# One of five convolution taps of fourteen gates made on ScalarE and added by an accumulating transfer

## The chip, the cores and the metric

The kernel runs on one core of one Trainium2 chip, with TensorE (PE), VectorE (DVE), ScalarE (ACT), GpSimd (POOL) and SyncE (SP) working from queues of their own. The metric is the device time of one launch in microseconds (us). Everything is float32.

## The reference

The first half is linear attention for 8 batches and 8 heads: kv = k^T v for each head, out = q kv, and each row of out is divided by its root mean square and scaled by g_norm. The heads side by side make x with 576 tokens and 512 channels a batch. The second half is a gated linear unit whose gate is a causal convolution over five tokens:

```
xp = np.concatenate([np.zeros((B, K - 1, D)), x], axis=1)      # K = 5
for k in range(K):
    gate_pre += conv_w[k][None, None, :] * xp[:, k:k + S, :]
gate = 1.0 / (1.0 + np.exp(-gate_pre))
val = x @ w_val
return gate * val @ w_out
```

## The kernel before, in words

The whole order of the work is written out by hand in a string, PLAN: 1151 steps such as `gate_tap 2 0 3`, each a small function, called one after the other. Every engine works its own instructions in that order, and waits by semaphores for what the others make. So a step that waits holds all that stands behind it on its engine.

For a batch b, k and v come by two half loads (SP's queue), and kv_product makes kv on TensorE. raw_pair (L500) and raw_product multiply q with it into PSUM, two chunks of 128 tokens at a time in one PSUM tile, `raws`, which the next pair writes again. square (L524, ScalarE) and sums (L533, VectorE) make the sums of squares, powers (L543, GpSimd) the inverse roots, and normalise (L564, ScalarE, eight instructions a chunk, L572) writes x, emptying the PSUM tile. turn_blocks (L600, VectorE) transposes x in 32x32 blocks, and move_blocks (L603) moves them by four transfers of 64 KB, issued by GpSimd at L608, into xT, where channels lie on partitions. There are two xT tiles, for even and odd batches. halo (L612, GpSimd) copies the four border columns that the convolution needs.

For each block jt of 128 channels there is then one gate, 128 partitions by 576 tokens, 288 KB, in one of three buffers:

- gate_start (L617, ScalarE): the tap of the current token, x times a weight a partition;
- gate_tap for taps 3, 2, 1 and 0 (L623, VectorE, one instruction at L625): gate = x shifted * weight + gate;
- gate_end (L630, ScalarE, L632): the sigmoid, in place;
- gated (L648, VectorE, L650): gv = gv * gate, which also sets the gate's buffer free.

Meanwhile TensorE makes x @ w_val. For batches 2 to 7 that is val_fast (L673), seven groups of products in three PSUM banks, with sums of x made by x_sums (L662, VectorE); val_keep (L691) copies or adds the banks into gv, by ScalarE (L696 to L708) or VectorE (L694). Some of the groups add to a bank that val_keep has just copied. The output products (out_product, L718 and L725; fast_product, L784) read gv, keep_out and fast_keep empty their banks, and store writes the result from SP's queue.

Transfers issued by GpSimd use eight semaphores in turn; one that takes a semaphore waits until the transfer eight before it has landed. The steps that the change touches stand in the plan like this, gate 2 of batch 2 as the example (dots for steps between):

```
x_sums 2 1; gate_start 2 2; normalise 3 4; gate_tap 2 2 3; ... gate_tap 2 2 2; ... gate_tap 2 2 1; ...
powers 4 3; ... load_half v 5 1; gate_tap 2 2 0; ... powers 4 2; ... gate_end 2 2; ... normalise 4 2; ... gated 2 2
```

Of the kernel before, what the change touches and what calls it, by code (L numbers as in the profile page):

```python
# [15 lines left out]
P = 128  # L16
# [3 lines left out]
load_q_rows 0 1; stage_weight cw 0; load_q_rows 0 0; load_half v 0 0; load_half k 0 0; load_half v 0 1;  # L20
load_half k 0 1; warm_up; stage_weight wval 1; stage_weight wval 0; start_warm 36; turn_q_rows 0 0;
turn_q_rows 0 1; narrow_weight cw 0 0; turn_q_rows 0 2; narrow_weight cw 0 1; narrow_weight cw 0 2; sort_q 0 0;
turn_q_rows 0 3; sort_q 0 1; turn_q_rows 0 4; narrow_weight cw 0 3; kv_product 0 0; sort_q 0 2;
load_q_rows 1 0; narrow_weight cw 0 4; narrow_weight cw 0 5; load_half k 1 0; sort_q 0 3; narrow_weight cw 0 6;
load_half v 1 0; narrow_weight cw 0 7; sort_q 0 4; load_q_rows 1 1; load_half k 1 1; stage_weight wval 2;
keep_warm 2; kv_product 0 1; stage_weight wval 3; turn_cw; load_half v 1 1; kv_copy 0; keep_cw;
narrow_weight wval 1 0; raw_product 0 3; load_half v 2 0; raw_product 0 2; square 0 3; raw_product 0 4;
sums 0 3; stage_weight wout 0; square 0 2; raw_product 0 1; square 0 4; powers 0 3; sums 0 2;
narrow_weight wval 1 1; sums 0 4; raw_product 0 0; load_half v 2 1; square 0 1; narrow_weight wval 0 0;
narrow_weight wval 0 1; powers 0 2; square 0 0; normalise 0 3; sums 0 1; turn_x 0 3; sums 0 0; keep_x 0 3;  # L30
powers 0 4; normalise 0 2; narrow_weight wval 1 2; narrow_weight wval 1 3; turn_x 0 2; normalise 0 4;
turn_q_rows 1 0; roots 0; keep_x 0 2; narrow_weight wval 0 2; turn_x 0 4; sort_q 1 0; turn_q_rows 1 1;
keep_x 0 4; narrow_weight wval 0 3; normalise 0 1; turn_q_rows 1 2; halo 0; sort_q 1 1; normalise 0 0;
turn_x 0 1; narrow_weight wval 1 4; kv_product 1 0; narrow_weight wval 0 4; keep_x 0 1; sort_q 1 2;
narrow_weight wval 0 5; turn_x 0 0; narrow_weight wval 1 5; narrow_weight wval 0 6; turn_q_rows 1 3;
keep_x 0 0; narrow_weight wval 0 7; gate_start 0 0; turn_q_rows 1 4; narrow_weight wval 1 6; kv_product 1 1;
sort_q 1 3; load_q 2 0; narrow_weight wval 1 7; gate_start 0 1; narrow_weight wval 2 0; val_product 0 0 1;
gate_start 0 2; narrow_weight wval 3 0; sort_q 1 4; load_q 2 1; gate_tap 0 2 3; kv_copy 1; gate_tap 0 0 3;
narrow_weight wval 3 1; raw_product 1 3; narrow_weight wval 2 1; gate_tap 0 1 3; load_half k 2 0;
raw_product 1 2; keep_val 0 0 1; gate_tap 0 0 2; square 1 3; narrow_weight wval 3 2; val_product 0 1 1;  # L40
sums 1 3; square 1 2; gate_tap 0 1 2; powers 1 3; narrow_weight wval 2 2; load_half k 2 1; gate_tap 0 2 2;
narrow_weight wval 2 3; stage_weight wout 2; raw_product 1 1; sums 1 2; narrow_weight wval 3 3;
narrow_weight wval 2 4; raw_product 1 0; keep_val 0 1 1; powers 1 2; square 1 1; narrow_weight wval 2 5;
normalise 1 3; val_product 0 0 0; load_q 2 2; gate_tap 0 0 1; sums 1 1; turn_q 2 0; normalise 1 2; powers 1 1;
turn_x 1 3; narrow_weight wval 3 4; val_product 0 1 0; narrow_weight wval 2 6; keep_x 1 3; load_q 2 3;
narrow_weight wval 3 5; square 1 0; narrow_weight wval 2 7; normalise 1 1; turn_x 1 2; sums 1 0;
raw_product 1 4; gate_tap 0 2 1; stage_weight wout 1; powers 1 0; kv_product 2 0; narrow_weight wout 0 0;
square 1 4; sums 1 4; narrow_weight wout 0 1; narrow_weight wval 3 6; kv_product 2 1; keep_x 1 2; turn_q 2 1;
powers 1 4; normalise 1 0; gate_tap 0 2 0; turn_x 1 1; load_q 3 0; val_product 0 2 1; narrow_weight wval 3 7;
keep_x 1 1; gate_tap 0 1 1; keep_val 0 1 0; narrow_weight wout 0 2; gate_tap 0 1 0; keep_val 0 0 0; turn_x 1 0;  # L50
normalise 1 4; gate_tap 0 0 0; val_product 0 2 0; narrow_weight wout 2 0; narrow_weight wout 0 3; keep_x 1 0;
narrow_weight wout 0 4; kv_copy 2; val_product 0 3 1; turn_q 2 2; keep_val 0 2 1; keep_val 0 2 0; turn_q 2 3;
narrow_weight wout 2 1; load_q 3 1; gate_end 0 0; narrow_weight wout 0 5; turn_x 1 4; narrow_weight wout 0 6;
raw_pair 2 3; keep_val 0 3 1; keep_x 1 4; gated 0 0; narrow_weight wout 2 2; stage_weight wout 3; halo 1;
val_product 1 0 1; narrow_weight wout 0 7; load_q 3 2; square 2 3; square 2 2; sums 2 3;
narrow_weight wout 2 3; sums 2 2; powers 2 3; gate_end 0 1; val_product 1 0 0; narrow_weight wout 1 0;
gate_end 0 2; narrow_weight wout 2 4; gate_start 0 3; gated 0 1; keep_val 1 0 1; narrow_weight wout 2 5;
powers 2 2; load_half v 3 1; val_product 1 1 1; normalise 2 3; gate_tap 0 3 3; load_half k 3 0;
load_half v 3 0; turn_q 3 0; narrow_weight wout 2 6; val_product 0 3 0; normalise 2 2; gated 0 2;
narrow_weight wout 2 7; turn_blocks 2 3; narrow_weight wout 1 1; load_q 3 3; raw_pair 2 1; gate_tap 0 3 2;  # L60
narrow_weight wout 1 2; narrow_weight wout 3 0; raw_product 2 4; keep_val 1 0 0; turn_q 3 1; square 2 1;
val_product 1 1 0; load_half k 3 1; keep_val 0 3 0; sums 2 1; narrow_weight wout 3 1; gate_tap 0 3 1;
square 2 0; powers 2 1; square 2 4; sums 2 0; narrow_weight wout 3 2; val_product 1 2 1; gate_tap 0 3 0;
keep_val 1 1 1; narrow_weight wout 1 3; turn_blocks 2 2; powers 2 0; narrow_weight wout 3 3;
narrow_weight wout 1 4; val_product 1 2 0; normalise 2 1; turn_q 3 2; narrow_weight wout 3 4; load_q 4 1;
normalise 2 0; narrow_weight wout 3 5; val_product 1 3 1; narrow_weight wout 3 6; sums 2 4; load_q 4 0;
keep_val 1 1 0; narrow_weight wout 3 7; powers 2 4; gate_end 0 3; turn_blocks 2 1; kv_product 3 0;
gate_start 1 0; narrow_weight wout 1 5; keep_val 1 2 1; gated 0 3; normalise 2 4; val_product 1 3 0;
narrow_weight wout 1 6; gate_start 1 1; gate_tap 1 0 3; narrow_weight wout 1 7; turn_x 2 4; kv_product 3 1;
turn_blocks 2 0; keep_x 2 4; gate_start 1 2; gate_tap 1 0 2; move_blocks 2 3; keep_val 1 3 0; out_product 0 1;  # L70
turn_q 3 3; load_half k 4 1; kv_copy 3; load_half k 4 0; gate_tap 1 2 3; keep_val 1 3 1; keep_val 1 2 0;
gate_tap 1 1 3; gate_tap 1 0 1; gate_tap 1 1 2; raw_pair 3 3; gate_tap 1 0 0; gate_tap 1 1 1; out_product 0 0;
square 3 3; move_blocks 2 2; gate_tap 1 2 2; keep_out 0 1; gate_end 1 0; store 0 1; sums 3 3; square 3 2;
gate_tap 1 2 1; gated 1 0; powers 3 3; load_q 4 2; sums 3 2; out_product 0 3; keep_out 0 0; gate_tap 1 1 0;
gate_start 1 3; gate_tap 1 2 0; powers 3 2; gate_end 1 1; gate_tap 1 3 3; normalise 3 3; gate_tap 1 3 2;
move_blocks 2 1; store 0 0; out_product 0 2; gate_tap 1 3 1; gate_end 1 2; normalise 3 2; gated 1 1;
gate_tap 1 3 0; load_half v 4 0; halo 2; gated 1 2; gate_end 1 3; val_sums 0; raw_pair 3 1; keep_out 0 2;
gated 1 3; keep_out 0 3; turn_blocks 3 3; store 0 2; raw_product 3 4; square 3 1; val_sums 1; out_product 0 5;
square 3 0; move_blocks 2 0; turn_q 4 0; load_half v 4 1; sums 3 1; turn_blocks 3 2; val_sums 2; powers 3 1;
load_q 4 3; sums 3 0; out_product 0 7; turn_q 4 1; keep_out 0 5; square 3 4; powers 3 0; turn_q 4 2;  # L80
load_q 5 0; normalise 3 1; weight_sums 0; sums 3 4; val_sums 3; powers 3 4; normalise 3 0; out_product 0 4;
turn_blocks 3 1; x_sums 2 0; x_sums 2 1; gate_start 2 2; normalise 3 4; gate_tap 2 2 3; gate_start 2 0;
turn_blocks 3 0; kv_product 4 0; turn_q 4 3; gate_tap 2 2 2; kv_product 4 1; x_sums 2 3; turn_x 3 4;
x_sums 2 2; kv_copy 4; load_half k 5 1; val_fast 2 0 0; store 0 5; gate_tap 2 2 1; keep_x 3 4; raw_pair 4 3;
move_blocks 3 3; val_keep 2 0 0; val_fast 2 0 1; store 0 3; square 4 3; square 4 2; sums 4 3; val_fast 2 0 2;
gate_start 2 1; sums 4 2; powers 4 3; val_fast 2 0 3; load_half k 5 0; gate_tap 2 1 3; val_keep 2 0 2;
# [773 lines left out]
```

## Time and profile before

| what | us |
|---|---|
| median of 2 runs | 314.65 (313.96 and 315.34) |
| span of the profiled execution, first to last instruction | 313.7 (the page gives no other time of it) |
| granted TensorE clock in it | 1.000 |
| one tap on VectorE (L625), mean of 128 | 0.810 |
| one gate_start on ScalarE (L619), mean of 32 | 0.796 |
| issue of one 64 KB move on GpSimd (L608), mean of 96 | 0.556 |
| landing of such a move after its issue, least / median / most | 1.9 / 3.4 / 7.7 |

The profile shows one execution. Times of instructions count from the start of the span. For each group of instructions it gives the busy time, the mean of one and the idle time of the engine before them. The chain is followed back from the last instruction, at each step to what released it. A timeline lists instructions in order of time, runs of alike ones merged.

### The profile page before, as it was taken

What the parts mean: (1) busy time and instruction counts of PE and PEld (TensorE: products, weight loads), DVE (VectorE), ACT (ScalarE), POOL (GpSimd) and SP (SyncE); (2) the same over time, 40 slices, a digit from 0 to 9 for tenths busy, and PEclk for the clock granted to TensorE, in tenths of its full rate; (3) what the DMA queues carried; (4) which work ended last, traced back from release to release, by engine and by line L of the source; (5) the groups of instructions that cost most, each with busy time, mean ns of one, the idle gap of its engine ahead of it and who ended that gap; (6) DMA issues with size and microseconds to landing.
All of it is one profiled execution on the core that took longest, in us unless ns stands there. A gap on an engine that the chain in (4) does not pass through costs nothing.

```text
span 313.7 us, 8362 instructions
## 1 busy us (share of the span) xinstructions
PE 302.8 (97%) x3197; PEld 217.6 (69%) x3197; DVE 255.7 (82%) x462; ACT 191.1 (61%) x542; POOL 133.4 (43%) x175
## 2 busy tenths in 40 slices
PE   7978999999999999999999999999999999999993
PEld 7866878777645485757666776587668868888582
DVE  1149899999999969899999899899998999764412
ACT  1457899999485867747685858485773343352120
POOL 3033073435588456666684659265749000000000
PEclk9999999999999999999999999999999999999999
DMA  7999597599677769668966986422335213022322
GB/s 276 377 386 352 149 294 219 173 298 239 186 189 210 210 188 342 196 168 276 270 155 194 251 251 160 118 50 54 100 78 127 58 25 88 0 67 57 89 73 85
DMA packets 26696, 55.50 MB, mean 177 GB/s; under 512 B 6166, under 2 KB 8214, under 8 KB 26656
## 3 DMA queue, kind: packets, MB, share of 16 engines
q1 hardware_dynamic: 22608, 46.61, 49.8%
q0 software_dynamic: 3168, 6.32, 7.9%
q10 hardware_dynamic: 880, 2.03, 1.9%
q8 instruction: 25, 0.41, 0.5%
q14 instruction: 15, 0.12, 0.1%
HBM read 39.21 MB, written 9.44 MB: 155 GB/s over the span
## 4 chain that ended last, share of the span: by engine, by line
PE 85%; ACT 5%; DMA 4%; DVE 2%; SPq 1%; issue 1%; POOL 1%; ACTq 0%; DVEq 0%
PE out L718 18%; PE va L687 15%; PE a L784 8%; PE vc L687 8%; PE cb L784 6%; PE val L637 6%; PE raw L438 5%; PE out L725 5%; PE raw L510 4%; PE vb L687 4%; PE qTps L472 3%; PE raw L493 2%; DMA k<-in_k_dram 2%; DMA qs<-in_q_dram 2%; PE xTps L587 1%; ACT x L572 1%
## 5 line engine op out<-in xcount | busy, mean ns | idle before, releaser
L625 DVE SCALAR_TENSOR_TENSOR gate<-xT,cwT,gate 128x576 f32<-128x576 f32 x128 | 101.0, 810 | 2.1 <-ACT gate L619 1.6
L546 POOL TENSOR_TENSOR rt<-ss,mhalf 128x8 f32<-128x8 f32 (+1 forms) x38 | 65.4, 1728 | 80.7 <-DVE ss L540 77.1
L608 POOL DMA_DIRECT2D xT<-y x96 | 52.8, 556 | 17.4 <-DVE xs L671 6.0
L718 PE MATMUL out<-wout,gv 128*128 128x512 f32 x128 | 57.3, 595 | 0.0
L572 ACT ACTIVATE x<-raw,rt 128x64 f32<-128x64 f32 x252 | 55.3, 369 | 2.2 <-POOL rt L546 1.6
L718 PEld LDWEIGHTS out<-wout,gv 128*128 128x128 f32 x128 | 23.9, 190 | 26.0 <-issue 24.1
L637 PE MATMUL val<-xT,wval 128*128 128x288 f32 x128 | 32.9, 409 | 0.1
L540 DVE TENSOR_REDUCE ss<-sq 128x8 f32<-128x520 f32 (+1 forms) x38 | 23.3, 626 | 8.3 <-ACT sq L528 8.1
L528 ACT ACTIVATE sq<-raw 128x512 f32<-128x512 f32 (+1 forms) x40 | 21.6, 564 | 12.4 <-PE raw L510 8.8
L637 PEld LDWEIGHTS val<-xT,wval 128*128 128x128 f32 x128 | 23.6, 190 | 6.3 <-ACT xT L594 0.3
L619 ACT ACTIVATE gate<-xT,cwT 128x576 f32<-128x576 f32 x32 | 25.2, 796 | 4.0 <-DVE gv L650 3.9
L687 PE MATMUL va<-xs,vsum 128*128 128x288 f32 x96 | 27.2, 406 | 0.0
L650 DVE TENSOR_TENSOR gv<-gv,gate 128x576 f32<-128x576 f32 x32 | 24.2, 762 | 3.0 <-ACT gate L632 2.8
L632 ACT ACTIVATE gate<-gate 128x576 f32<-128x576 f32 x32 | 22.1, 702 | 5.5 <-DVE gate L625 5.4
L687 PEld LDWEIGHTS va<-xs,vsum 128*128 128x128 f32 x96 | 18.2, 190 | 4.7
L733 ACT COPY ot<-out 128x512 f32<-128x512 f32 x20 | 12.0, 603 | 14.0 <-PE out L725 6.0
L438 PEld LDWEIGHTS raw<-v,k 64*64 64x64 f32 x1008 | 15.5, 135 | 4.7 <-issue 3.8
L793 DVE TENSOR_TENSOR ot<-cb,ot 128x256 f32<-128x256 f32 x16 | 6.7, 420 | 14.7 <-ACT ot L797 7.0
L615 POOL COPY xT<-xT 128x124 f32<-128x124 f32 x32 | 13.4, 456 | 10.3 <-ACT xT L594 10.3
L708 ACT COPY gv<-va 128x288 f32<-128x288 f32 x12 | 4.8, 400 | 19.8 <-PE va L687 19.8
L438 PE MATMUL raw<-v,k 64*64 64x64 f32 x1008 | 16.8, 220 | 0.0
L600 DVE STREAM_TRANSPOSE y<-x 128x512 f32<-128x512 f32 x24 | 16.7, 698 | 0.0
(119 smaller groups left out, 516.7 us busy)
## 6 DMA issues: line engine op xcount, KB each, us to landing
qs<-in_q_dram SPq DMA_DIRECT2D x96, 140.0 KB, 4.3
out_dram<-ot SPq DMA_DIRECT2D x140, 64.0 KB, 2.3
k<-in_k_dram SPq DMA_DIRECT2D x14, 576.0 KB, 6.5
v<-in_v_dram SPq DMA_DIRECT2D x12, 576.0 KB, 6.3
xT<-y POOLq DMA_DIRECT2D x96, 64.0 KB, 3.4
y<-in_moe_w_val_dram SPq DMA_DIRECT2D x4, 512.0 KB, 12.0
w_wout<-in_moe_w_out_dram SPq DMA_DIRECT2D x4, 512.0 KB, 7.2
qs<-in_q_dram SPq DMA_DIRECT2D x3, 576.0 KB, 5.4
```

Of the source, the lines that this page charges most:

```text
L438: nc.tensor.matmul(raws[r * D:(r + 1) * D, s, i * D:(i + 1) * D], st["k", b, i][rows, r, cols], st["v", b, i][rows, r, cols], start=(j == ...
L540: nc.vector.reduce_sum(out=ss[:, 0:n], in_=st["sq", b, c][:, 0:n], axis=AX.X)
L546: nc.gpsimd.tensor_tensor(out=rt[:, 0:n], in0=st["ss", b, c][:, 0:n], in1=mhalf[:, 0:n], op=ALU.pow)
L572: nc.scalar.activation(out=x[:, to * D:(to + 1) * D], in_=one, func=AF.Copy, scale=st["rt", b, c][:, h:h + 1])
L608: nc.gpsimd.dma_start(out=xTs[b % 2][i * TB:(i + 1) * TB, :, first:first + P], in_=y[a * TB:(a + 1) * TB, i])
L619: nc.scalar.activation(out=gate[:], in_=xTs[b % 2][:, jt, HALO:SX], func=AF.Copy, scale=cwT[:, K - 1, jt:jt + 1])
L625: nc.vector.scalar_tensor_tensor(out=gate[:], in0=xTs[b % 2][:, jt, tap * TB:tap * TB + S], scalar=cwT[:, tap, jt:jt + 1], in1=gate[:], op ...
L637: nc.tensor.matmul(val[:], wval[:, kc, jt * P:(jt + 1) * P], xTs[b % 2][:, kc, HALO + n * SV:HALO + (n + 1) * SV], start=(kc == 0), stop=( ...
L650: nc.vector.tensor_tensor(out=both, in0=both, in1=st["gate", b, jt][:], op=ALU.mult)
L687: nc.tensor.matmul(st[bank, "val", b, mj][:], weights_[:, k], tokens()[:, k], start=(n in (0, 1, 3) and k == 0), stop=(k == NK // 2 - 1), ...
L718: nc.tensor.matmul(po[:], gv[:, jt, first:first + P], wout[:, jt, :], start=(jt == 0), stop=(jt == NK - 1),)
L784: nc.tensor.matmul(st[bank, i, p], tokens()[:, k], weights_[:, k], start=(n < 2 and k == 0), stop=(k == NK // 2 - 1), skip_group_check=True)
```

## The change

For fourteen of the 32 gates (2/2, 2/0, 3/2, 3/0, 4/2, 4/3, 4/1, 5/2, 6/2, 6/1, 6/0, 7/2, 7/1, 7/3, written batch/block) the last tap, tap 0, is no longer an instruction of VectorE. Right behind gate_start, a new step gate_side makes x shifted by four tokens times tap 0's weight on ScalarE, into a tile of its own (`side`, three buffers). A second new step, gate_add, is a transfer issued by GpSimd that adds the side tile to the gate in SBUF.

```
+    def gate_side(b, jt):
+        st["side", b, jt] = side = work.tile([P, S], FP32, tag="side", bufs=3, name=f"side{b}_{jt}")
+        nc.scalar.activation(
+            out=side[:], in_=xTs[b % 2][:, jt, 0:S], func=AF.Copy, scale=cwT[:, 0, jt:jt + 1])
+
+    def gate_add(b, jt):
+        nc.gpsimd.dma_start(out=st["gate", b, jt][:], in_=st["side", b, jt][:], accum_op=ALU.add)
```

In the plan, for the eleven gates of batches 2, 3, 4, 5 and 7, gate_add stands where gate_tap ... 0 stood, behind the gate's other taps:

```
-... gate_start 2 2; ... load_half v 5 1; gate_tap 2 2 0; load_half v 5 0; powers 4 2; ...
+... gate_start 2 2; gate_side 2 2; ... load_half v 5 1; gate_add 2 2; load_half v 5 0; powers 4 2; ...
```

For the three gates of batch 6 it stands right behind gate_side, ahead of the other taps:

```
-... gate_start 6 0; fast_product 2 1 4; ... gate_tap 6 0 3; ... gate_tap 6 0 2; ... gate_tap 6 0 1; ... gate_tap 6 0 0; ...
+... gate_start 6 0; gate_side 6 0; gate_add 6 0; fast_product 2 1 4; ... gate_tap 6 0 3; ... gate_tap 6 0 2; ... gate_tap 6 0 1; ...
```

On GpSimd's queue this puts gate_add 2/2 between powers 4/3 and powers 4/2; 2/0 between move_blocks 3/2 and 3/1; 3/2 and 3/0 together between move_blocks 4/2 and 4/1; 4/3 and 4/2 together between powers 6/1 and 6/0; 4/1 between powers 6/4 and halo 5; 5/2 between move_blocks 6/0 and powers 7/1; 6/2 and 6/1 behind halo 6 and ahead of move_blocks 7/3; 6/0 between move_blocks 7/2 and 7/1; and the three of batch 7 at the end. All other steps stand in the order in which they stood.

## The prediction

> **What bounds the kernel now.** I read the page's busy table first, then the busy time of one long stretch, then the groups of the instructions that the change touches, and last the places where its new waits would stand.
>
> The page says which engine fills the span:
>
> ```profile
> PE 302.8 (97%) x3197; PEld 217.6 (69%) x3197; DVE 255.7 (82%) x462; ACT 191.1 (61%) x542; POOL 133.4 (43%) x175
> ```
>
> The busy table of one stretch (columns: stretch, length, busy time of PE, PEld, DVE, ACT and POOL, granted clock, DMA share, GB/s) makes it sharper:
>
> ```profile
> 58.00:289.00 231.00, 230.88 (x2283) 159.95 (x2276) 211.38 (x353) 146.79 (x431) 116.68 (x154) 1.00 0.58 161
> ```
>
> From 58 to 289 us TensorE works 230.88 of 231.00 us at full clock. All fourteen changed gates lie in this stretch. Time that VectorE saves there can give back 0.12 us at most; time that TensorE is made to wait is paid in full, since its queue is in order and it has no idle time to catch up with. So the question is only whether the new steps make TensorE wait.
>
> The groups that are removed and added, or have the nearest kin:
>
> ```profile
> L625 DVE SCALAR_TENSOR_TENSOR gate<-xT,cwT,gate 128x576 f32<-128x576 f32 x128 | 101.0, 810 | 2.1 <-ACT gate L619 1.6
> L608 POOL DMA_DIRECT2D xT<-y x96 | 52.8, 556 | 17.4 <-DVE xs L671 6.0
> L619 ACT ACTIVATE gate<-xT,cwT 128x576 f32<-128x576 f32 x32 | 25.2, 796 | 4.0 <-DVE gv L650 3.9
> ```
>
> **Part 1, VectorE.** Fourteen taps of 0.810 us go: 11.3 us off an engine that is 82% busy. Worth 0 to 0.12 us, by the stretch above. In the tail (289 to 313.7 us) there is no gate any more.
>
> **Part 2, ScalarE.** gate_side is gate_start with another slice: 14 x 0.796 = 11.1 us more. In each case the engine's own timeline has an idle wait for TensorE soon behind it that takes it up: 2.83 us before 111.16 for gates 2/2 and 2/0, 1.18 before 141.43 and 1.02 before 145.63 for batch 3, 1.02 before 175.36, 1.37 before 182.68 and 1.54 before 187.47 for batch 4, 0.97 before 210.00 for 5/2, 0.97 before 233.77 and 2.23 before 245.84 for batch 6, 2.69, 1.33 and 0.87 before 259.36, 262.25 and 276.81 for batch 7. I cost it at 0. Were one cover gone, the price would be one pitch, about 0.7 us.
>
> **Part 3, issue on GpSimd.** gate_add names 128 contiguous pieces (one a partition), as a move does (32 partitions, 4 pieces each), so 14 x 0.556 = 7.8 us on an engine that is 43% busy; if the second operand's read doubles it, 1.1 us each. Queued behind it are powers (ScalarE's normalise waits for them) and the moves of the next batch's x. Gate 2/2's puts powers of 4/2 0.6 us later; its user starts at 120.99, 2.4 us after the old end. The two of batch 4 (4/3, 4/2) put powers of 6/0 some 1.1 us later and the add of 4/1 to about 194.7 us. The add of 6/1 waits for its side (about 233.8) and holds the move of 7/3 for 2.5 us; the add of 6/0 waits for its side at about 243.8 (its gate buffer comes free at 242.2) and puts the last moves of batch 7 to about 248.7. They land by 252; the first reader starts at 255.55. All hidden, with SP's queue untouched.
>
> **Part 4, the new wait, which decides.** The sigmoid (gate_end, ScalarE) now waits for the landing instead of a tap, and in batch 6 the first VectorE tap waits for it. The trace has no accumulating transfer. From below, a landing takes 1.9 us (the quickest 64 KB move); from above, the 512 KB weight loads in the page's list take 12.0 us. How long a GpSimd-issued SBUF-to-SBUF transfer takes depends on where it stands, as the moves issued in four stretches (118 to 123, 148 to 153, 160 to 163, 194 to 196 us) show:
>
> ```profile
> L608 POOL DMA_DIRECT2D xT<-y x8: 548/548/599, 118.5 to 122.4; - x8
> DMA to landing us min/median/max: 5.0/5.3/6.1
> ...
> L608 POOL DMA_DIRECT2D xT<-y x8: 548/548/593, 148.7 to 152.5; - x8
> DMA to landing us min/median/max: 3.7/6.9/7.7
> ...
> L608 POOL DMA_DIRECT2D xT<-y x4: 548/550/599, 161.0 to 162.7; - x4
> DMA to landing us min/median/max: 1.9/2.0/2.0
> ...
> L608 POOL DMA_DIRECT2D xT<-y x4: 548/548/592, 194.0 to 195.7; - x4
> DMA to landing us min/median/max: 3.0/3.4/3.6
> ```
>
> Quiet 2.0, under loads 5 to 7.7. The loads of the first stretch are in SP's queue just ahead, and no move lands until they are through:
>
> ```profile
> 115.71 0.43 SPq L303 DMA_DIRECT2D k<-in_k_dram  x1
> 116.19 1.00 SPq L303 DMA_DIRECT2D v<-in_v_dram  x2
> ```
>
> A gate is 288 KB against the move's 64. Between 112 and 126 us the 576 KB k load takes 3.7 us to land, a 64 KB store 2.3 in the page: 1.4 us for 512 KB more, so 0.6 for 224 KB more, and 1.2 if reading the destination doubles it. I take the local row plus 1.2 us. Place by place:
>
> Gate 2/2. GpSimd reaches it after the first of two powers, at 116.9 us. Landing 116.9 + 5.3 + 1.2 = 123.4. The sigmoid starts at 120.41 now, so ScalarE stands 3.0 us, and behind it eight normalise steps of 4/2 that empty the PSUM tile that raw_pair writes next:
>
> ```profile
> 120.41 0.70 ACT L632 ACTIVATE gate<-gate 128x576 f32<-128x576 f32 x1
> 120.99 1.75 ACT L572 ACTIVATE x<-raw,rt 128x64 f32<-128x64 f32 x8
> ...
> 123.28 0.78 ACT L619 ACTIVATE gate<-xT,cwT 128x576 f32<-128x576 f32 x1 [0.54 <-DVE gv L650]
> ```
>
> The chain has that product at 123.18 us, straight behind the output product, 0.4 us after 122.74:
>
> ```profile
> 119.60 3.58 PE out L725 x16
> 123.18 1.09 PE raw L510 x64
> ```
>
> So TensorE pays 3.0 - 0.4 = 2.6 us (bounds: 0 for a landing within 3.5 us; 5 for one of 9).
>
> Gate 2/0: issue 124.0, sigmoid 128.9, and 1.6 us of margin behind that (the last normalise of that group ends at 133.6, the next k-v product starts at 135.2): 0.
>
> Gates 3/2 and 3/0 stand one behind the other behind a four-part move: issued at 150.9 and at 152.0 (3/0's last remaining tap). With the local median, 152.0 + 6.9 + 1.2 = 160.1, and 161.3 if the first one's 1.2 us is added too. The sigmoids start at 156.10 and 157.07; the copy of a PSUM bank behind the second ends at 158.14 and TensorE adds to that bank from 158.68, so about 0.5 us is free. Stand 3.0 to 4.2 us, TensorE pays 2.5 to 3.7: I take 3.2 (bounds 0 and 8).
>
> Batch 4: 4/3 and 4/2 are issued at about 188 in a quiet queue; 5 us until their sigmoids: 0. 4/1: 194.7 + 3.4 + 1.2 = 199.3 against 197.53; 1.8 us, of which about 1.1 is margin (behind gated 4/1, the x sums of batch 5 end at 203.0 and TensorE reads them at 204.1): 0.7 (bounds 0 and 3).
>
> Batch 5: issue 223.05, sigmoid 227.87: 0. Batch 6: sides done at 228.7, 233.8, 243.8, first taps at 232.5, 236.9 and 246.9, about 3.1 us each against 3.2 to 4.1 us: up to 1 us of VectorE, partly paid by taps that are gone: 0.5 (bounds 0 and 5). Batch 7: 8 us and more between add and sigmoid: 0.
>
> Sum 2.6 + 3.2 + 0.7 + 0.5 = 7.0 us.
>
> The rule against the row: the Trainium skill (DMA: Bandwidth & Descriptors, Anatomy of one DMA, SWDGE path) fits a transfer issued by GpSimd by 2.0 us plus bytes over 436 GB/s, for a gate an estimate of 2.7 us. The quiet row of 2.0 us agrees with it, the rows under loads do not. By the rule alone every gate but a few tenths in batch 6 lands in time and the sum would be 0. The same page (Queues, rings and completion order) has each DMA engine take turns between queues packet by packet, which would favour that; the moves of 118.5 us, none landed before 124, speak against equal turns.
>
> The profiled execution has a span of 313.7 us, 0.9 under the median of the runs, 314.65; the page gives no other time of it. 314.65 + 7.0 = 321.6 us.
>
> **Rivals.** (a) Hidden: the transfers get in between the loads and land within 3.5 us (2/2) and 5.5 us (3/0). That is the point from which nothing waits; all else is covered and the time stays 314.65, from 314.0 to 315.3. For it speak the quiet rows; against it the two busy rows, taken at the very places. It is the case that is not slower; the time cannot fall much below, by the 0.12 us.
> (b) The accumulation itself is slow: a landing of 10 to 12 us under load and 6 in the quiet. Then 2/2 costs 5, batch 3 6 to 8, 4/1 3, batch 6 three VectorE stands of nearly 3 us, about 5 in all: 19 to 21 us, 334 us or more. For it: two reads and a write for each byte, of which the trace shows nothing. Against it: the engines move 64 KB in 2.0 us when quiet.
> (c) GpSimd's issue is the dear part: at 2 us each instead of 0.56, powers of 4/2 and of 6/0 come 1.5 to 3 us later; 2/2's user has 2.4 us, 6/0's normalise ends 2.0 us before the k-v product at 193.71, so 1 to 2 us on top of (a): 316. Against it: 548 ns in nearly every one of 96 rows.
>
> **Numbers.** The forecast (late landings at two or three places, 317.5 to 327) 0.58; (a) 0.20; (b) 0.15; (c) 0.07. The range that should hold 8 in 10 goes from 315.0, which leaves out about half of (a), to 333, which leaves out most of (b). A run of this kernel tells a difference of about 2%, 6.3 us, from none. Faster by more: 0.01, since TensorE leaves nothing to gain. Slower by more than 320.9: a bit over half of the forecast's cases and all of (b), 0.51. Within: 0.48.
>
> **What would show it.** Right: gate_end on ScalarE waits for a DMA in the list of waits, 2 to 4 us near 120 and twice near 157; TensorE gaps before raw_pair 4/1 and in batch 3's val products; TensorE's busy sum unchanged near 302.8 and the span longer by the gaps. VectorE's taps 114 instead of 128, its busy time 11 us less and its idle time longer. Wrong: landings of gate transfers under 4 us in batches 2 and 3 (then a), over 9 (then b), or GpSimd rows of the new transfer over 1 us (then c). A gap of TensorE at a place that I cost at 0 would break part 2 or 3.

## The result, and the profile after

The changed kernel takes 331.43 us, the median of 2 runs (330.33 and 332.53), against 314.65: a ratio of 1.054, 95% interval 1.044 to 1.065. The forecast was +7.0 us; it is +16.8. The profiled execution took 330.33 us, of which the span is 328.2, and its mean clock is 0.984 where it was 1.000. (Line numbers, such as L626 for the sigmoid, are those of each run's own kernel.)

The busy table of the page:

```profile
PE 305.2 (93%) x3197; PEld 217.3 (66%) x3197; DVE 246.1 (75%) x448; ACT 199.6 (61%) x556; POOL 148.0 (45%) x189
```

VectorE has 9.6 us less to do and ScalarE 8.5 more, somewhat less than the 11.3 and 11.1 foreseen, but TensorE, which has the same 3197 instructions, now leaves 23.0 us of its span unused, where it left 10.9, and needs 2.4 us more for them. From the groups (columns as before: instructions, then busy time and mean ns, then idle time ahead and its releaser) and the page's lists of the clock and of landings:

```profile
PEclk9999999999999995999979999999999999999999
...
L611 DVE SCALAR_TENSOR_TENSOR gate<-xT,cwT,gate 128x576 f32<-128x576 f32 x114 | 89.9, 809 | 2.9 <-DMA gate<-side 1.6
...
L622 POOL DMA_DIRECT2D gate<-side x14 | 13.3, 969 | 44.9 <-ACT gate L626 10.4
...
L626 ACT ACTIVATE gate<-gate 128x576 f32<-128x576 f32 x32 | 22.0, 698 | 17.0 <-DMA gate<-side 13.2
...
gate<-side POOLq DMA_DIRECT2D x14, 288.0 KB, 4.6
```

The sigmoid (L626) waits 13.2 us for landings, which the tap never made it do. The list of waits says how that is spread: five times, the longest 6.1 us.

```profile
ACT gate L626 <- DMA gate<-side: 13.2, 5, 6.1
```

The clock row has two dips, in the 16th and 21st of its 40 slices. The longest wait, gate 2/2's, lies just ahead of the first. ScalarE's timeline there:

```profile
118.13 0.59 ACT L727 COPY ot<-out 128x512 f32<-128x512 f32 x1
124.80 0.68 ACT L626 ACTIVATE gate<-gate 128x576 f32<-128x576 f32 x1 [6.08 <-DMA gate<-side]
125.39 1.73 ACT L558 ACTIVATE x<-raw,rt 128x64 f32<-128x64 f32 x8
```

and the chain of work, which now runs through the transfer:

```profile
114.96 9.82 DMA gate<-side
...
124.80 0.02 ACT gate L626
...
125.39 1.74 ACT x L558 x8
...
127.17 1.98 PE raw L496 x64
```

The transfer is issued at 114.96 and lands 9.82 us later. The sigmoid, the eight normalise steps behind it and the product that needs their PSUM tile follow in single file. The last line holds a second loss: these 64 products took 1.09 us before and take 1.98 now. The busy times by stretch (columns: stretch, length, busy time of PE, PEld, DVE, ACT and POOL, granted clock, DMA share, GB/s) show why:

```profile
120.70:124.10 3.40, 0.68 (x4) 0.00 (x0) 0.09 (x1) 0.00 (x0) 0.00 (x0) 1.00 1.07 292
124.10:127.50 3.40, 0.33 (x12) 0.33 (x16) 1.99 (x3) 2.70 (x10) 0.00 (x0) 0.50 0.90 271
127.50:130.90 3.40, 3.40 (x74) 2.81 (x67) 1.11 (x3) 1.85 (x4) 3.31 (x6) 0.50 0.98 251
```

After a stretch of 3.4 us in which TensorE hardly worked, the granted clock is 0.50 for the next, and after that one, hardly used either, for one more.

Laying the starts of TensorE's 3197 instructions, which come in the same order in both traces, one against the other gives the loss by place: 2/2 costs 7.5 us (5.8 of standing and 1.7 of half clock), batch 3 costs 5.7 (3.9 of standing and 1.8 of half clock, which lasts 3.4 us from 168.5), batch 4 costs 1.9, batch 6 costs 1.2. The sum is 16.3. (The expectations below have 7.3, 5.4 and 16.1 for it.) The span grew by only 14.5, because in this execution TensorE left the half clock of its start 1.7 us sooner; other executions do that without the change.

### The profile page after: what moved, and what is told of

Its sections match the earlier page's. It is cut to its first block, busy times and chain, and to the rows that moved or that the text cites. A ratio compares the mean times of both kernels' runs of the same rounds, so it can differ in the third digit from the quotient of the medians.

```text
span 328.2 us, 8386 instructions
## 1 busy us (share of the span) xinstructions
PE 305.2 (93%) x3197; PEld 217.3 (66%) x3197; DVE 246.1 (75%) x448; ACT 199.6 (61%) x556; POOL 148.0 (45%) x189
## 4 chain that ended last, share of the span: by engine, by line
PE 62%; DMA 11%; ACT 7%; DVE 7%; POOL 5%; issue 5%; SPq 1%; DVEq 0%; POOLq 0%; ACTq 0%
PE va L681 11%; PE out L712 10%; PE a L778 8%; DMA gate<-side 7%; PE val L631 6%; PE cb L778 6%; PE vc L681 5%; PE raw L424 4%; DMA qs<-in_q_dram 3%; PE qTps L458 3%; POOL rt L532 3%; PE vb L681 2%; PE out L719 2%; PE raw L496 2%; POOL xT L594 2%
## 5 line engine op out<-in xcount | busy, mean ns | idle before, releaser
L532 POOL TENSOR_TENSOR rt<-ss,mhalf 128x8 f32<-128x8 f32 (+1 forms) x38 | 66.8, 1764 | 80.2 <-DVE ss L526 76.9
L611 DVE SCALAR_TENSOR_TENSOR gate<-xT,cwT,gate 128x576 f32<-128x576 f32 x114 | 89.9, 809 | 2.9 <-DMA gate<-side 1.6
L594 POOL DMA_DIRECT2D xT<-y x96 | 56.7, 745 | 10.4 <-DVE y L586 7.2
L622 POOL DMA_DIRECT2D gate<-side x14 | 13.3, 969 | 44.9 <-ACT gate L626 10.4
L626 ACT ACTIVATE gate<-gate 128x576 f32<-128x576 f32 x32 | 22.0, 698 | 17.0 <-DMA gate<-side 13.2
L681 PE MATMUL va<-xs,vsum 128*128 128x288 f32 x96 | 28.2, 417 | 3.8 <-ACT gv L694 3.7
L496 PEld LDWEIGHTS raw<-kvbd,qT 64*64 64x64 f32 x768 | 13.2, 142 | 13.0 <-ACT x L558 7.1
L496 PE MATMUL raw<-kvbd,qT 64*64 64x64 f32 x768 | 15.0, 229 | 6.9 <-ACT x L558 5.8
L601 POOL COPY xT<-xT 128x124 f32<-128x124 f32 x32 | 16.4, 664 | 10.3 <-ACT xT L580 10.3
L727 ACT COPY ot<-out 128x512 f32<-128x512 f32 x20 | 11.8, 602 | 13.2 <-PE out L712 4.4
```

The lines of the kernel that those rows point to most:

```text
L496: nc.tensor.matmul(st["raw", b, x][cols, r, hp * D:(hp + 1) * D], st["qT", b][rows, hp, x * P + half * D:x * P + (half + 1) * D], kv_bd[b ...
L532: nc.gpsimd.tensor_tensor(out=rt[:, 0:n], in0=st["ss", b, c][:, 0:n], in1=mhalf[:, 0:n], op=ALU.pow)
L594: nc.gpsimd.dma_start(out=xTs[b % 2][i * TB:(i + 1) * TB, :, first:first + P], in_=y[a * TB:(a + 1) * TB, i])
L611: nc.vector.scalar_tensor_tensor(out=gate[:], in0=xTs[b % 2][:, jt, tap * TB:tap * TB + S], scalar=cwT[:, tap, jt:jt + 1], in1=gate[:], op ...
L681: nc.tensor.matmul(st[bank, "val", b, mj][:], weights_[:, k], tokens()[:, k], start=(n in (0, 1, 3) and k == 0), stop=(k == NK // 2 - 1), ...
```

## The experiments

Theory A: the price is lateness. The transfers of 2/2 and 3/x land late because of the loads beside them, TensorE stands, and the clock halves behind long gaps. Theory B: the accumulation costs by itself, wherever it is. Theory C: the price is the added work of ScalarE and GpSimd.

**e1, the same ScalarE work, no transfer.**

```
-nc.gpsimd.dma_start(out=gate, in_=side, accum_op=ALU.add)
+nc.vector.tensor_tensor(out=gate, in0=gate, in1=side, op=ALU.add)
```

> gate_side stays on ScalarE in all fourteen gates, but VectorE adds the side tile (one tensor_tensor where the tap stood), so no transfer and no new wait on a landing. Theory A (the landing comes late: ScalarE stands at the sigmoid, TensorE loses that time, and after a long gap runs at half clock for a while): the loss goes, 314.7 us within 1.5, no TensorE gap over 0.5 us behind 60 us. Rival C (the 11 us of new ScalarE work costs): 5 us or more stay, 320 or above.

315.15 us against 314.31, ratio 1.001 (0.998 to 1.005), clock 1.0, no gap. Fourteen sides on ScalarE cost nothing measurable; the loss belongs to the transfer, its issue on GpSimd included.

**e2, a plain copy in the accumulation's place.**

```
-    accum_op=ALU.add)
+    )
```

> The transfer copies the side tile over the gate and does not add, so what the earlier taps put there is left out of the result; places, sizes and waits are those of the changed kernel. Theory A: a copy has one read less, its packets cost about half of 195 ns, so it lands 1 to 2 us earlier, but still behind the loads: the gap near 121 us shrinks from 5.8 to about 4, the one near 164 from 3.7 to 1 to 3; 322 to 329 us. Rival B (the accumulation makes the landing late): no gap, 314 to 316.

321.58 us, ratio 1.022 (1.009 to 1.035), just under the 322 to 329 expected. Its group, to be laid beside the 969 ns above:

```profile
L622 POOL DMA_DIRECT2D gate<-side x14 | 8.0, 568 | 43.9 <-ACT gate L626 10.7
```

A copy of 288 KB goes as 64 packets of 4608 bytes at 178 ns, the accumulation as 128 of 2304 bytes at 195 ns: spread over 16 engines 0.7 against 1.6 us of work. In quiet places the landings are 2.3 to 2.4 us and 3.4 to 3.6. At 2/2 they are 6.4 and 9.8, at 3/2 and 3/0 6.7 and 7.7 against 8.4 and 8.75. So the accumulation adds about 1.1 us in the quiet and 1.1 to 3.4 at these three places beside the loads. TensorE loses 7.3 us with the copy and 16.3 with the accumulation: what comes on top falls where no margin is left, and stretches of half clock come to 10.2 us in all instead of 3.4.

**e3 and e4, one place at a time.** e3 gives batches 2 and 3 their four taps again, e4 changes gate 2/2 alone.

```
e3: -gate_side 2 2; 2 0; 3 2; 3 0      their gate_add -> gate_tap ... 0
e4: -gate_side of all but 2 2          their gate_add -> gate_tap ... 0
```

> The four gates of batches 2 and 3 have their four taps again; the other ten are as changed. By the shift of TensorE's instructions between the two traces these two batches hold 7.3 and 5.4 of 16.1 us. Theory A: about 3.3 us stay, 317 to 319.5 us, and the clock stays at full since no gap is over 1 us. Rival C (cost spread over all gates as work): 10 of 14 parts stay, about 326.

> Only gate 2/2 is changed, the other thirteen have their taps. Theory A: one gap of 5 to 6 us before raw_pair 4/1 and a stretch at half clock behind it that costs 1 to 2 more: 321 to 323 us. Rival C (one fourteenth of the work): 315 to 316.

e3: 318.31 us, ratio 1.011 (1.002 to 1.021), no half clock. e4: 323.00 us, 1.026 (1.019 to 1.034), landing 9.5 us, gap 5.5, half clock for 6.8 us. TensorE's delays are 3.6 and 7.8 us. With the 5.7 us of batch 3 that makes 17.1, against 16.3 for all at once: the places add up within 0.8 us.

**e9, the covered places alone.** Gates 4/3, 4/2, 5/2, 7/2, 7/1, 7/3 changed, the other eight as before.

> Only six of the fourteen gates are changed: 4/3, 4/2, 5/2, 7/2, 7/1 and 7/3, the ones whose landing in the changed kernel came before anybody needed it; the other eight have four taps again. A (a landing costs only where it ends a wait): no gap of TensorE over 0.3 us behind 40 us, time within 0.3% of the kernel before. B (accumulating transfers take time from the loads or from VectorE wherever they run, 0.3 to 0.5 us each): 316.5 to 317.5 us. A gain would be VectorE's six taps, 4.2 us, if any of its time were on the path; theory A says none of it is.

314.92 us against 315.00, ratio 1.000 (0.998 to 1.002). Six accumulating transfers, landing 3.5 to 6.4 us after their issue, cost nothing measurable, and VectorE's six taps fewer gain nothing. From 56 to 287 us TensorE is as full as it was before (columns as above):

```profile
56.00:287.00 231.00, 230.87 (x2287) 159.64 (x2286) 206.78 (x350) 151.12 (x437) 122.52 (x160) 1.00 0.62 169
```

Theory B falls, and with it theory C for GpSimd's issue of these six.

**e5 and e6, two first tries at 2/2.** e5 issues its transfer earlier; e6 moves the three loads of batch 5 in the plan.

```
e5: gate_tap 2 2 1; +gate_add 2 2; ... powers 4 3; ... -gate_add 2 2
e6: -load_half k 5 0; v 5 1; v 5 0 ... gate_end 2 2; +load_half k 5 0; v 5 1; v 5 0
```

> All fourteen gates as changed, but GpSimd issues gate_add 2/2 right behind VectorE's tap 1 of that gate, ahead of powers 4/3, some 4 us earlier. Theory A (the landing is late because the transfer stands behind the three loads issued at 114 to 115 us): it is ahead of them, lands before the sigmoid, and the 7.3 us of batch 2 go: 322 to 325 us. Rival B (an accumulating transfer needs 9 to 10 us here whatever is ahead of it): issued 4 us earlier it still lands about 2 us late, gap near 2 us, 325 to 328.

> All fourteen gates as changed, gate_add 2/2 at its place, but the three loads of batch 5 (k half 0, both halves of v) stand in SP's queue behind the sigmoid of 2/2; their product starts some 15 us later, so they have room. Theory A: the transfer has a free way, lands 3.5 to 5 us after its issue at about 115 to 117 us, at most 1.5 us of gap and full clock: 322.5 to 325.5 us. Rival B: landing after 8 us or more still, no change from 331.

Both missed theory A's times: 330.05 us (1.046, 1.040 to 1.051) and 332.04 (1.052, 1.048 to 1.057). In e5, 2/2 lands after 6.5 us and its gap is gone, but the loss comes back one gate later. The chain of e5:

```profile
124.19 8.06 DMA gate<-side
...
132.28 0.68 ACT gate L639
132.96 3.29 ACT x L571 x16
...
136.29 2.31 PE raw L437 x140
138.61 2.43 issue
```

Gate 2/0's transfer, covered in the changed kernel by the delay that 2/2 had caused, is now the late one; it lands 8.06 us after its issue, and the k-v product of batch 5 waits for the normalise steps behind its sigmoid. The 2.43 us of "issue" inside that product are something else (last section). In all, batch 2 costs 4.2 us instead of 7.5, but batch 3 costs 6.1 and batch 4 3.8, where a stretch of half clock now falls. e6 did not do what it was for: gate_end is a step of ScalarE, and does not hold SP's queue. The loads were issued at 116.2 to 117.2 us, the transfer at 116.35: still side by side, and it landed after 8.8 us.

**e10 and e11, 2/2 alone, out of the loads' way.** e10 is e4 with e5's early place; e11 is e4 with the three loads behind the first four q loads in SP's queue. (These loads are 576 KB each, as the page's list has them; the sizes given in the expectations of e11 and e13 are half of what they are.)

```
e10: gate_tap 2 2 1; +gate_add 2 2; ... powers 4 3; ... -gate_add 2 2
e11: -load_half k 5 0; v 5 1; v 5 0 ... load_q 5 1; +load_half k 5 0; v 5 1; v 5 0
```

> Only gate 2/2 is changed, and its transfer is issued right behind the tap 2 2 1, ahead of two of the three loads of batch 5, as in the run that moved it for all fourteen gates. There it landed 6.5 us after its issue, TensorE had no gap at 2/2, and what was saved came back as gaps of 1.4 and 2.4 us behind gate 2/0, whose own transfer landed 8.1 us after its issue. A (the landing of 2/2 behind the loads, then the half clock): with 2/0 back on four taps nothing is late, no gap over 0.3 us, 314.3 to 315.3 us. If the early place only shifts the loss to other work (the moves of batch 3 behind it on GpSimd, the loads), the gaps stay and the time is 318 to 320 us.

> Only gate 2/2 is changed, with its transfer where the change puts it; the three loads of batch 5, 864 KB, stand behind the first four q loads in SyncE's queue, so that they are issued some 8 us later than the transfer, not beside it (the earlier try at this put them only 2 us later, still beside it). A (the loads keep the transfer's packets back): the first packet starts 1.5 to 2 us after the issue, not 4.95, the landing takes 4 to 5.5 us, not 9.5, the gap before raw is under 1.2 us and no stretch of half clock follows: 314.5 to 316.5 us, unless the later loads make kv_product of batch 5 wait, which would show as a gap before raw<-v,k. If the loads are not what holds it, the first packet still starts 4 to 5 us after the issue, and the time is 321 to 323 us.

e10: 315.24 us against 315.00, ratio 1.002 (0.999 to 1.005); landing 5.8 us, and one gap of 0.8 us, over the 0.3 expected, inside the k-v product of batch 5 (last section). e11: 317.66, 1.010 (1.006 to 1.014); landing 3.75 us where e4 has 9.5, with the transfer itself and its place unchanged, no gap at 2/2 and no half clock. The landing in e4, then in e11:

```profile
DMA to landing us min/median/max: 9.5/9.5/9.5
...
DMA to landing us min/median/max: 3.8/3.8/3.8
```

Of the expected 314.5 to 316.5 e11 misses the top by 1.2; its trace has a gap of 1.3 us inside the k-v product of batch 5. The DMA view of the changed kernel, from 0.5 us behind the issue to the transfer's first packet, has only the loads' queue:

```profile
q1 hardware_dynamic: 602, 1.31, 93.4%
...
gate<-side POOLq DMA_DIRECT2D x1, 288.0 KB, 9.8
```

and from there to the end of the transfer's packets the loads' queue still has nearly half of the engines' time:

```profile
q0 software_dynamic: 255, 0.53, 58.4%
q1 hardware_dynamic: 301, 0.57, 47.6%
```

In e11 the first 3.9 us behind the issue look like this:

```profile
q0 software_dynamic: 151, 0.32, 46.2%
q8 instruction: 1, 0.02, 1.4%
q1 hardware_dynamic: 17, 0.01, 0.6%
```

q0 is GpSimd's queue, q1 SP's. The first packet starts 1.5 us after the issue in e11 and 5.0 in the changed kernel. Those 3.5 us of waiting beside the loads, and packets that then take 4.0 us instead of 1.8, make 5.7 of the 6.1 us between the landings. Theory A holds for 2/2.

**e7 and e8, the gap without the transfer.** The kernel before, with nine or five idle copies on ScalarE ahead of the sigmoid of 2/2.

```
+hold 9;   (e8: hold 5)   gate_end 2 2
```

> The kernel before with nothing of the change; ScalarE makes nine idle copies (128x576, on a tile of their own, 6.1 us in all) ahead of the sigmoid of 2/2, so it stands about as long as it stood for the landing. Theory A with the clock (a long gap of TensorE brings half clock by itself): a gap of 5.5 to 6 us, then 3.4 to 6.8 us at half clock, 7 to 8 us more than before: 321.5 to 323. Rival (the clock falls because of the transfers or of the load on the chip): only the gap, 5.5 to 6 us, clock full: 320 to 320.7.

> As e7 with five idle copies (3.4 us): a gap of about 3.0 us. If a gap shorter than 3.4 us can bring half clock, as one of 2.4 us seems to have done with the plain transfers and one of 2.6 us not, the loss is 4.5 to 5 us; if not, 3.0 us: 317.3 to 319.5.

322.09 us (1.021, 1.016 to 1.025) and 319.14 (1.011, 1.005 to 1.018). Stretches of e7:

```profile
121.30:124.70 3.40, 0.12 (x2) 0.00 (x0) 0.00 (x0) 3.24 (x6) 0.00 (x0) 1.00 1.06 328
124.70:128.10 3.40, 0.78 (x28) 0.78 (x32) 2.40 (x4) 3.23 (x11) 0.00 (x0) 0.50 0.88 253
128.10:131.50 3.40, 3.40 (x59) 2.67 (x52) 1.96 (x4) 1.58 (x3) 0.65 (x1) 0.50 0.66 178
```

and of e8:

```profile
121.60:125.00 3.40, 0.56 (x36) 0.56 (x40) 2.17 (x3) 3.40 (x11) 0.00 (x0) 1.00 0.99 292
125.00:128.40 3.40, 3.40 (x54) 2.67 (x44) 2.42 (x5) 1.63 (x4) 0.89 (x1) 0.50 0.85 258
```

No transfer was added here, and the clock halves all the same, for 6.8 us after a gap of 5.9 and 3.4 us after one of 3.0. Against the kernel before, TensorE's delay behind the gap grows by a further 1.9 and 1.6 us. A stand of TensorE as long as 2/2's costs more than its length, whatever causes it.

**e12 and e13, batch 3.** e12 changes gate 3/2 alone; e13 does too, and moves two loads of batch 6 behind the next four q loads.

```
e13: -load_half v 6 0 ... -load_half k 6 1 ... load_q 6 2; +load_half v 6 0; k 6 1
```

> Only gate 3/2 is changed. In the changed kernel its transfer and that of 3/0 are issued 1.7 us apart, share the engines, and land 8.4 and 8.75 us after their issues; TensorE then has a gap of 3.7 us and a stretch of half clock. If the two transfers in a row make each other late: alone 3/2 lands within 6.5 us and the gap is under 1.5 us, 314.7 to 316.2 us. If the loads and the four moves beside them are enough: it lands after 8 us or more, with a gap of over 1.6 us and a half clock behind it, 317 to 320 us.

> Only gate 3/2 is changed, as in the run before that left it alone, where its transfer landed 7.4 us after its issue, first packet after 3.1 us, and TensorE had a gap of 1.5 us. Here the two loads of batch 6 beside it, 576 KB, stand behind the next four q loads in SyncE's queue. A (the loads keep the packets back): first packet 1.5 to 2.2 us after the issue, landing 4 to 5.5 us, the gap under 0.6 us, 314.5 to 316 us. If it is the moves on GpSimd's own queue, four of 64 KB ahead of it, or the q loads that make it late, the landing stays over 6.5 us and the gap over 1 us, 317 to 321 us.

e12: four runs from 317.21 to 322.01 us against a median of 315.00, ratio on record 1.019 (1.015 to 1.023), about 1.013 without the longest. The quickest was profiled: a landing of 7.4 us, a gap of 1.5 and no half clock, which lies between the two outcomes expected. So most of 3/2's lateness is there without 3/0. e13: 315.74 us against 315.13, ratio 1.002 (0.999 to 1.005). The source view of the transfer, in e12 and then in e13:

```profile
  ACT gate L638: 2.1, 1
...
DMA to landing us min/median/max: 7.4/7.4/7.4
```

```profile
  ACT gate L638: 0.8, 1
...
DMA to landing us min/median/max: 6.1/6.1/6.1
```

The loads made up 1.3 us of the lateness and nearly all of the price. The landing is still 6.1, not the 4 to 5.5 expected. Whether the moves of x on GpSimd's own queue or the q loads keep the rest was not tested.

**e14, the whole change with both groups of loads moved.**

```
e11's and e13's moves of load_half, on the changed kernel
```

> The whole change, all fourteen gates, with both groups of loads moved back in SyncE's queue as in the two runs that did so for one gate: the three of batch 5 behind the first q loads, the two of batch 6 behind the four q loads that follow them. By theory A 2/2 lands in time, which takes back its 7.3 us, and 3/2 comes 2 to 3 us sooner, which brings the gap of batch 3 under 2 us; what stays is 1 to 1.5 us in kv_product of batch 5, up to 4 us at 2/0, whose own transfer becomes the late one, 1.5 to 2.5 us in batch 3 where 3/0 follows 3/2, and 3.3 us in batches 4 and 6: 320 to 325 us. If the accumulating transfers cost by their number and not by the loads beside them, 328 to 332 us.

326.81 us, ratio 1.038 (1.034 to 1.042), beyond the 320 to 325 expected. 2/2 lands in 3.85 us, 3/2 and 3/0 in 5.5 and 6.55, and batch 3 costs 1.8 us, not 5.7. But the loads that left 2/2 now stand beside 2/0, as its landing of 9.1 us shows (first packet after 4.6): TensorE has gaps of 2.8 and 0.75 us at the k-v product with half clock for 3.4 us between, about 5 us. Moving the loads moves the lateness. Nothing here beats the kernel before.

## Why the prediction was wrong

- **Parts 1 and 2 were right.** ScalarE's fourteen sides cost nothing (e1), and six of VectorE's taps are worth nothing (e9). One of the waits listed as cover, 0.97 us before 210.00, is for GpSimd and not for TensorE; 5/2 cost nothing all the same.
- **Part 3 was right.** The record of one issue is 0.969 us long, not 0.556, and two in batch 4 exceed the bound of 1.1 (1.17 and 1.51). But these records overlap with what follows: GpSimd's next instruction starts 0.6 us behind the issue (114.96 and 115.62 at 2/2, 205.63 and 206.28 at 4/1), so what stands behind it is held by about the price taken. e9 shows it hidden for six gates.
- **Part 4 failed at the step "I take the local row plus 1.2 us".** For 2/2 it gave a landing of 6.5 us after the issue; the runs show 9.8 and 9.5, with 6.4 for a plain copy. These 3.3 us are what lies between the 2.6 us taken and the gap of 5.8. Both terms of the step were too small. The wait: the local row belongs to 64 KB moves issued some 2 us later beside the same loads; their first packet started 3.2 us after the first issue, the transfer's after 5.0. The size: behind the first packet the step leaves 3.3 us, and the transfer took 4.8, since its packets started over 3.8 us beside loads that took half of the engines' time, where they need 1.5 in the quiet. The 1.2 us came from a k load's 3.7 us; the two v loads of 576 KB right behind it in the same view have a median of 6.4. Held against the plain copy of e2, which landed near the 5.9 us that the step would give for it, the accumulation beside the loads costs 3.4 us; the step had 0.6 for it. For 3/2 and 3/0 the step gave 8.1 to 9.3 us and they landed after 8.4 and 8.75: right, and the standing of 3.9 us is near the 3.2 taken.
- **A term was missing altogether: the clock.** Each of the two long stands brought TensorE 1.7 to 1.8 us more at half clock, 3.5 us in all. e7 and e8 show it without any transfer. The sum had TensorE pay for waiting, never for having waited; the sign "busy sum unchanged near 302.8" failed by it (305.2). The Trainium skill (TensorE: Matmul & The Clock Gate, Part 1: The HAM clock gate) has a free-running window of 3413 ns after which an idle TensorE falls to half rate; the 3.41 and 6.83 us of the records agree. Its section on why this matters for kernels warns of idle gaps over about 3 us. My own upper bound for 2/2 was a gap of 5; the two side by side would have put the term into the range.
- **The small places:** batch 4 cost 1.9 us where 0.7 was taken (4/1 landed after 5.9, not 4.6), batch 6 cost 1.2 instead of 0.5. That is 1.9 us too little in all; what made these landings late was not tested apart.
- **2/0, costed at 0, was 0 only because 2/2 had already held TensorE up.** With 2/2 in time, its landing of 8 to 9 us makes a gap of 1.4 us in e5 and of 2.8, with half clock behind it, in e14. The prediction counted 4.9 us to the sigmoid and 1.6 of margin; its own price for that stretch, 5.3 plus 1.2, uses that up to the last tenth.
- **The rivals.** (b) came near the time, 334 against 331.4, for another reason: the landing of about 10 us is there at 2/2 alone, and only beside the loads. In the quiet it is 3.5, not 6. Its 5 us for 2/2 were also too few by the prediction's own arithmetic, where 5 stands for a landing of 9 us, not of 10 to 12. That 331.4 lies inside the range up to 333 is luck: this part was there for (b), and the forecast itself ended at 327. (a) is what e9, e10 and e13 give, when the loads are out of the way.

Term by term, half clock included: 7.5 us instead of 2.6 at 2/2, 5.7 instead of 3.2 in batch 3, 1.9 instead of 0.7 in batch 4, 1.2 instead of 0.5 in batch 6; 16.3 instead of 7.0.

## What to carry to other kernels

Before you hand an engine's step to a transfer, look at what the loads' queue issues within the two or three microseconds around it, and price the landing with a wait beside those loads (3.5 us more than in the quiet here) and packets at about half speed; the same 288 KB took 3.75 us or 9.5 by that alone. Where TensorE fills the span and would stand for about half of a clock window (some 1.6 to 2 us here), add the half-speed stretch to the price. And check the places you cost at zero once more as if the larger losses ahead of them were gone.

## What the runs showed of the hardware that was not expected

**The clock goes by windows on a fixed grid, not by the length of a gap.** In every trace the changes of the clock lie whole multiples of 3.413 us apart. Cut each run into stretches of that length on these edges. Leaving out the first 20 us and the last 15, TensorE stood for 1.56 us or more within one such stretch in 20 cases over all the profiled executions; behind 18 of them the next stretch ran at 0.50, behind two (1.65 and 1.68 us) it did not. Shorter stands, up to 1.44 us, had no effect. In the last 15 us stands of 1.73, 1.91 and 1.99 us had none either, so the bound is not sharp: it lies somewhere from 1.5 to 2 us. The copy of e2 shows both sides. At 123 us a gap of 2.4 us fell into one window; at 162.7 one of 2.6 us fell across an edge, and TensorE was busy for about 2 us in either half:

```profile
123.20:126.60 3.40, 1.07 (x64) 1.02 (x64) 2.11 (x3) 2.94 (x10) 0.64 (x2) 1.00 1.00 299
126.60:130.00 3.40, 3.40 (x21) 2.48 (x14) 2.54 (x4) 1.58 (x3) 3.38 (x5) 0.50 0.92 255
160.70:164.10 3.40, 1.99 (x9) 1.21 (x7) 2.17 (x3) 0.97 (x2) 3.40 (x5) 1.00 1.04 303
164.10:167.50 3.40, 2.18 (x9) 1.76 (x10) 2.28 (x4) 3.20 (x12) 2.68 (x7) 1.00 1.00 228
```

A gap well under the skill's 3 us (same page) is thus enough if it lies within one window, and the same gap can cost 1.6 us or nothing. That may be why e12's runs spread from 317.2 to 322.0: the quickest had a mean clock of 0.997, the other three 0.981 to 0.989. Only the quickest was profiled.

**GpSimd's transfer got no turn beside a run of loads.** For 3.5 us after the 1.5 us in which a first packet starts in the quiet, 2/2's transfer got none, and the loads kept 93.4% of the engines' time. At 127.6 us in the same run, beside q loads of 140 KB that took about 90%, 2/0's first packet started after 1.8 us. Whether the transfer's packets stood ready and were passed over, and what it is about the 576 KB loads that does this, was not tried.

**TensorE stood inside one k-v product, with no releaser,** 140 matmuls into 144: 0.8 us in e10, 1.3 in e11, 2.4 in e5. A 16 KB packet of the instruction queue started at 136.0, 135.9 and 138.6 us in these traces, and TensorE went on 2.5 to 2.7 us behind its start each time; in the kernel before it started at 134.6, 2.7 us ahead of that place, and there was no such gap. That the matmuls waited for their own code is argued from this, not shown.
